# Matmuls whose result is not read: 512 columns in one instruction for four of 128 columns

## The chip, the cores and the metric

One core of a Trainium2 chip runs the whole program in one launch. The metric is the device time of one execution in microseconds (us). TensorE appears in the profile as PE (matmuls) and PEld (the loads of their stationary operand), VectorE as DVE, ScalarE as ACT, GpSimd as POOL, SyncE, which issues most transfers, as SP.

## The reference

Attention over 8 batches of 8 heads (576 tokens, 64 dims each) with a window of 32, plain for heads 0 to 3 and dilated by 4 for heads 4 to 7, and behind it a mixture of 8 experts: each token goes to the expert with the highest logit.

```python
scores = scale * np.matmul(q, k.transpose(0, 1, 3, 2))
scores = np.where(masks[None, :, :, :], scores, -1000000000.0)
scores = scores - np.max(scores, axis=-1, keepdims=True)
attn = np.exp(scores)
attn = attn / (np.sum(attn, axis=-1, keepdims=True) + 1e-09)
attn_out = np.matmul(attn, v)
...
x = attn_out.transpose(0, 2, 1, 3).reshape(B * S, H * D)      # 4608 x 512
logits = x @ w_gate
expert_idx = np.argmax(logits, axis=1)
gate_w = softmax(logits)[np.arange(N), expert_idx]
...
for e in range(E):
    h = np.maximum(x_sorted[lo:hi] @ w1[e], 0.0)              # 512 -> 1024
    y_sorted[lo:hi] = h @ w2[e]                               # 1024 -> 512
return gate_w[:, None] * y_sorted[inv_perm]
```

Everything is float32. No matmul that this change touches has a result that enters the output.

## The kernel before, in words

The work is cut into units of two heads of one batch (32 units). A unit runs through these steps: q and k are loaded and turned by DVE (lines 581 to 596), PE makes the scores block by block (line 659), DVE scales and masks them out of PSUM (line 679) and takes the smallest (691), ACT makes the exponentials and their sums (700), DVE inverts the sums (710, 712), POOL multiplies (716), PE turns the weights (726), ACT or DVE copies them to SBUF as eT (983), and PE multiplies by v (753, 764) into a tile xo that ACT or DVE copies to xT (775, 777). After a batch, a routing stage makes logits (1068, 1082), ranks (1112, 1115) and token rows (1045), and POOL writes the rows to a bucket in DRAM (527). The experts' work follows: some slots of 128 tokens early, between the units of later batches (first layer line 1475, second layer 1491), and after the last batch pairs of slots (lines 1604 to 1640), three single slots and 14 short ones (1742, 1769).

No engine's queue follows the written order of the code. A planner (class Plan) holds all steps with a cost, an engine, the buffers taken and a rank, and emits them one at a time; the order it makes is then pinned for each engine. The planner also models TensorE's clock, and where PE would sit idle before a step it puts matmuls in whose result is not read. It works out how many (m, at most 12) from the idle time and the constant FILL = 0.22 us for each, sets plan.owed = m, and calls ahead(name) when a PSUM tile is free early:

```python
m = max(min(self.MOST, int(idle / us)), self.WARMING if cold and begin < at else 0)
if m > 0:
    self.owed, self.free[e] = m, begin
    if name:
        self.fill(name)
```

The function unread(to) (line 804) emits the owed matmuls: each multiplies the constant tile idle (128x128 ones, written by POOL on line 801) by itself into the first 128 columns of the PSUM tile that the next real step will write. It is called with a fresh tile by bank (line 544), two_banks (729) and ahead (809). The planner stops filling when the first expert slot comes (plan.until), so all of these matmuls lie in the first 118 us. In the trace they stand under line 806, with the names scores, ahead, xo and weights of the tile written.

The kernel's 86 unread matmuls stand in 26 runs of 1 to 12: 12, 12, then runs of 1 to 3, then one of 11, one of 7, one of 4, and runs of 1 to 3 between and after.

Of the kernel before, what the change touches and what calls it, by code (L numbers as in the profile page):

```python
# [357 lines left out]
def kernel(  # L358
# [10 lines left out]
    nc = tc.nc  # L369
# [168 lines left out]
    coming = {}  # L538

    def banks(tag, name):  # L540
        n, bufs = (1024, 1) if tag == "two" else (512, 2)
        return psum.tile([128, n], F32, tag=tag, name=name, bufs=bufs)

    def bank(name, *dims, tag="misc"):
        t = coming.pop(tag, None) or banks(tag, name)
        unread(t[:, 0:128])
        if len(dims) < 2:
            return t[:, 0 : dims[0]] if dims else t
        return t[:, 0 : dims[0] * dims[1]].rearrange("p (a b) -> p a b", a=dims[0])
# [48 lines left out]
    def turn_pe(p, n, m):  # L598

        tp = bank("turned", 6, 64)  # L600
        for c in range(6):
            for r in range(2):
                rows = slice(64 * r, 64 * r + 64)
                nc.tensor.matmul(
                    tp[rows, c], lhsT=raws[p][rows, RUN * n + 6 * m + c], rhs=ident[rows, rows],
                    start=True, stop=True,
                )
        return tp
# [21 lines left out]
    def scores(i, banks):  # L630

        sc = [[bank("scores", tag=t) for t in two] for two in banks]
        parts = [heads_qk(i + u) for u in range(len(sc))]
        G = len(parts[0][0])
# [88 lines left out]
    def weights(ev, g):  # L723
        tp = bank("weights", 4, 128)
        for c in range(3):
            nc.tensor.transpose(tp[0:KB, c], ev[:, 3 * g + c], ident)  # L726
        return tp

    def two_banks(name):
        two = coming.pop("two", None) or banks("two", name)  # L730
        unread(two[:, 0:128])
        return two.rearrange("p (h x) -> p h x", h=2)

    def summed(eT, ty, hp):
        half_s = S // 2
        xo = two_banks("xo")
        if ty == 1:
            for n in range(NB + 1):
# [44 lines left out]
    for i in range(2):  # L783
        a = E * CAP + 128 * i
        wrote_bucket(nc.gpsimd.dma_start(bucket[a : a + 128], blank), 0)
    plan = Plan(0.7)
# [13 lines left out]
    idle = cpool.tile([128, 128], F32, name="idle")  # L800
# [1 line left out]
    plan.others = [(name, ring[name]) for name in ("slot", "two", "s")]  # L802

    def unread(to):
        for _ in range(plan.owed):
            nc.tensor.matmul(to, lhsT=idle, rhs=idle, start=True, stop=True)
        plan.owed = 0

    def ahead(name):
        if name not in coming:  # L810
            coming[name] = banks(name, "ahead")
        unread(coming[name][:, 0:128])

    plan.fill = ahead

# [206 lines left out]
    def route(b, hx, parts, other):  # L1022
# [15 lines left out]
        def to_rows(g):  # L1038

            pv = two_banks("xrow").rearrange("p h (g t x) -> p h t g x", g=4, t=2)  # L1040
            tiles = range(2 * g, min(2 * g + 2, NT))
            for i in tiles:
                for h in range(2):
                    for ty in range(2):
                        nc.tensor.transpose(
                            pv[:, i - 2 * g, ty].rearrange("p (h g) (r x) -> p h r g x", h=2, r=2)[:, h],
                            xT[:, 2 * ty + h, TT * i : TT * i + TT],
                            ident,
                        )
            R["pv", g] = pv  # L1050
# [12 lines left out]
        def parts_of_logits():  # L1063

            lp = two_banks("lp")[:, :, 0 : PAD // 2]
            for g in range(2):
                for c in range(4):
                    nc.tensor.matmul(
                        lp[32 * c : 32 * c + 32, g], lhsT=gate_w[:, c],
                        rhs=xT[:, c, PAD // 2 * g : PAD // 2 * g + PAD // 2],  # L1070
                        start=True, stop=True,
                    )
            R["lp"] = lp
# [1237 lines left out]
```

## Time and profile before

| | us |
|---|---|
| median of 3 runs | 731.18 |
| lowest, highest | 730.61, 737.0 |
| the profiled execution, its own time | 732.32 |
| its span, first to last instruction | 730.5 |
| mean granted TensorE clock | 0.981 |

A run of the same program can differ from the next by several us (730.61 to 737.0). The profiled execution lies 1.14 us above the median, and 1.82 us of its time lie outside its span. Times in rows are counted from the start of the span. In a row of a timeline, the first number is the start and the second the length of a group of like instructions; "[2.89 <-issue]" is idle time of the engine in front of it in which it waited for nothing that the profile shows. A float32 matmul of this kernel leaves two records on PE and two on PEld: line 1491 runs 88 times in the code and has 176 records.

### The profile page before, as it was taken

The numbers are of one execution on the slowest core, as the hardware profiler recorded it, in microseconds if no ns is written. First come the engines' busy times: TensorE is split into PE (matmuls) and PEld (weight loads), VectorE is DVE, ScalarE is ACT, GpSimd is POOL, SyncE is SP. The second block draws the span as 40 slices with busy tenths as digits, with TensorE's granted clock in tenths as the row PEclk, the third lists the DMA queues.
The fourth block names the chain that finished last, engine by engine and source line by source line (L and its number), as shares of the span: only waits on it lengthen the run. The fifth ranks groups of instructions, "written<-read, shape, count | busy, mean of one in ns | idle before, by whom it ended". The sixth has DMA issues, their size and how long they took to land. (4 is left out here: it accounts for less than half of the span.)

```text
span 730.5 us, 21652 instructions
## 1 busy us (share of the span) xinstructions
PE 696.5 (95%) x8520; PEld 584.0 (80%) x8520; DVE 431.7 (59%) x963; ACT 285.9 (39%) x906; POOL 283.1 (39%) x461
## 2 busy tenths in 40 slices
PE   5789999899999999999999999999999999999996
PEld 4678888768778678767987898878989887889894
DVE  7788877767777531754576555417565653455640
ACT  2598877748777764211120211211211212211210
POOL 1135254225343435356064352452542512552511
PEclk9699999999999999999999999999999999999999
DMA  9999977956676985184979569775997759965301
GB/s 267 331 268 313 346 195 209 319 164 177 154 172 156 262 273 185 62 305 99 395 201 348 163 210 395 217 245 157 373 372 223 222 179 385 401 244 198 131 20 48
DMA packets 117326, 171.32 MB, mean 235 GB/s; under 512 B 45628, under 2 KB 69950, under 8 KB 116704
## 3 DMA queue, kind: packets, MB, share of 16 engines
q1 hardware_dynamic: 109712, 149.55, 65.9%
q0 software_dynamic: 6352, 19.69, 7.2%
q8 instruction: 69, 1.13, 0.7%
q10 hardware_dynamic: 1152, 0.61, 0.3%
q14 instruction: 41, 0.34, 0.2%
HBM read 196.27 MB, written 20.22 MB: 296 GB/s over the span
## 5 line engine op out<-in xcount | busy, mean ns | idle before, releaser
L700 ACT ACTIVATE e<-e,lo 128x96 f32<-128x96 f32 x288 | 104.1, 368 | 11.9 <-DVE lo L691 11.9
L716 POOL TENSOR_TENSOR e<-e,rec 128x864 f32<-128x864 f32 x32 | 52.4, 1637 | 103.9 <-DVE rec L712 76.3
L1491 PE MATMUL py<-w,h 128*128 128x512 f32 x176 | 83.8, 611 | 0.9 <-issue 0.9
L1475 PE MATMUL ph<-xt,w 128*128 128x128 f32 x672 | 81.5, 276 | 0.0
L1475 PEld LDWEIGHTS ph<-xt,w 128*128 128x128 f32 x672 | 78.2, 192 | 2.5 <-issue 2.1
L659 PE MATMUL scores<-kT,qT 32*64 32x96 f32 (+2 forms) x2168 | 57.9, 257 | 15.0 <-issue 8.7
L527 POOL DMA_INDIRECT bucket<-rows,idx x40 | 39.4, 985 | 76.5 <-issue 13.9
L659 PEld LDWEIGHTS scores<-kT,qT 32*64 32x64 f32 (+2 forms) x2168 | 48.1, 134 | 22.8 <-issue 17.1
L1491 PEld LDWEIGHTS py<-w,h 128*128 128x128 f32 x176 | 31.6, 193 | 31.1 <-issue 30.6
L679 DVE SCALAR_TENSOR_TENSOR e<-scores,cst 128x384 f32<-128x384 f32 x122 | 43.9, 397 | 20.0 <-PE scores L659 8.6
L700 ACT ACTIVATION_READ_ACCUMULATOR e<-e,lo 128x1 f32 x288 | 55.6, 193 | 0.0
L1678 POOL DMA_INDIRECT out_dram<-y,top x22 | 24.5, 1112 | 79.4 <-ACT y L1659 75.0
L1604 POOL TENSOR_TENSOR v<-w 128x1024 f32<-128x1024 f32 x11 | 27.5, 2498 | 71.1 <-PE late_two L1629 63.7
L983 ACT COPY eT<-weights 96x384 f32<-96x384 f32 x94 | 42.0, 479 | 23.3 <-PE weights L726 19.9
L726 PE MATMUL weights<-cst,e 128*96 128x128 f32 x288 | 45.4, 285 | 3.1 <-POOL e L716 1.1
L1659 ACT ACTIVATE y<-y,gtp 128x512 f32<-128x512 f32 x22 | 15.0, 717 | 81.4 <-DVE y L1640 81.3
L726 PEld LDWEIGHTS weights<-cst,e 128*96 128x96 f32 x288 | 31.3, 131 | 15.6 <-issue 6.7
L1623 PE MATMUL pp<-late_rows,v 128*128 128x128 f32 x352 | 43.3, 276 | 0.0
L1623 PEld LDWEIGHTS pp<-late_rows,v 128*128 128x128 f32 x352 | 41.0, 192 | 1.2 <-issue 0.8
L1629 PE MATMUL pp<-w,h 128*128 128x256 f32 x176 | 41.9, 381 | 0.0
L1640 DVE TENSOR_TENSOR y<-pp,y 128x256 f32<-128x256 f32 x44 | 18.6, 423 | 39.4 <-PE pp L1629 35.2
L1640 DVE TENSOR_TENSOR h<-late_two,h 128x512 f32<-128x512 f32 x11 | 7.6, 688 | 57.0 <-PE late_two L1623 57.0
(223 smaller groups left out, 1454.2 us busy)
## 6 DMA issues: line engine op xcount, KB each, us to landing
w<-in_moe_w_dram SPq DMA_DIRECT2D x40, 2048.0 KB
raw<-in_moe_w_dram SPq DMA_DIRECT2D x42, 1024.0 KB
qT<-in_moe_w_dram SPq DMA_DIRECT2D x28, 512.0 KB
w<-in_moe_w_dram SPq DMA_DIRECT2D x8, 1024.0 KB
raw<-in_q_dram SPq DMA_DIRECT2D x14, 576.0 KB
raw<-in_k_dram SPq DMA_DIRECT2D x14, 576.0 KB
v<-in_v_dram SPq DMA_DIRECT2D x7, 864.0 KB
xT<-bucket SPq DMA_DIRECT2D x44, 128.0 KB
```

The source lines that it names most:

```text
L527: nc.gpsimd.indirect_dma_start(out=bucket, out_offset=bass.IndirectOffsetOnAxis(ap=idx, axis=0), in_=rows, in_offset=None, bounds_check=NR ...
L659: nc.tensor.matmul(two[r][row : row + rows, KB * c : KB * c + KB], lhsT=qs, rhs=ks, start=g == 0, stop=g == G - 1,)
L679: nc.vector.scalar_tensor_tensor(out=to, in0=at, scalar=-SCALE, in1=of, op0=OP.mult, op1=OP.add,)
L700: nc.scalar.activation(out=ev[:, c], in_=ev[:, c], func=AF.Exp, bias=lo[:, c : c + 1], scale=-1.0, accum_out=den[:, c : c + 1],)
L716: nc.gpsimd.tensor_tensor(out=ev, in0=ev, in1=rec.unsqueeze(2).broadcast_to([128, NC, KB]), op=OP.mult)
L726: nc.tensor.transpose(tp[0:KB, c], ev[:, 3 * g + c], ident)
L983: copier(e)(S_["eT"][:, 3 * g : 3 * g + 3], S_["w", g][0:KB, 0:3])
L1475: nc.tensor.matmul(ph[:, f % 4], lhsT=w1s[wbuf[j[0:2]]][:, c, 128 * f : 128 * f + 128], rhs=xt[:, c], start=c == 0, stop=c == 3,)
L1491: nc.tensor.matmul(py, lhsT=h[:, f], rhs=w2s[wbuf[j[0:2]]][:, f], start=f == 0, stop=f == 7)
L1604: (nc.gpsimd if engine == "POOL" else nc.vector).tensor_tensor(out=to, in0=a, in1=b, op=OP.subtract)
L1623: nc.tensor.matmul(to[:, f], lhsT=w[:, c, 128 * f : 128 * f + 128], rhs=x[:, c], start=c == 0, stop=c == 1,)
L1629: nc.tensor.matmul(to[:, 0:256], lhsT=x[:, f], rhs=w[:, f], start=f == 0, stop=f == 3)
```

## The change

unread emits plan.owed // 4 matmuls of 512 columns, whose moving operand is the tile idle read four times by a stride of zero, and then plan.owed % 4 of the old ones of 128 columns. The callers hand over 512 columns of the tile instead of 128. The planner's counts and costs are as they were.

```diff
@@ bank @@
-        unread(t[:, 0:128])
+        unread(t[:, 0:512])
@@ two_banks @@
-        unread(two[:, 0:128])
+        unread(two[:, 0:512])
@@ unread @@
     def unread(to):
-        for _ in range(plan.owed):
-            nc.tensor.matmul(to, lhsT=idle, rhs=idle, start=True, stop=True)
+        four = idle.unsqueeze(1).broadcast_to([128, 4, 128])
+        for _ in range(plan.owed // 4):
+            nc.tensor.matmul(
+                to.rearrange("p (a b) -> p a b", a=4), lhsT=idle, rhs=four, start=True, stop=True
+            )
+        for _ in range(plan.owed % 4):
+            nc.tensor.matmul(to[:, 0:128], lhsT=idle, rhs=idle, start=True, stop=True)
         plan.owed = 0
@@ ahead @@
-        unread(coming[name][:, 0:128])
+        unread(coming[name][:, 0:512])
```

Only runs of four and more change: five of the 26. On DVE, ACT, POOL and SP every instruction stands where it stood. On PE, the head of the program (scores and ahead are the tiles written, kT and qT the turned k and q, cst the constants, e and eT the weights before and after they are turned, v_71 a part of v):

```order
L806 MATMUL scores<-idle 128x128 x12
L659 MATMUL scores<-kT_70,qT 64x96 x72
L806 MATMUL ahead<-idle 128x128 x12
L659 MATMUL scores<-kT_70,qT 64x96 x64
L659 MATMUL scores<-kT_70,qT 32x96 x16
L726 MATMUL weights<-cst,e 96x128 x12
```

```order
L807 MATMUL scores<-idle 128x512 x3
L659 MATMUL scores<-kT_70,qT 64x96 x72
L807 MATMUL ahead<-idle 128x512 x3
L659 MATMUL scores<-kT_70,qT 64x96 x64
L659 MATMUL scores<-kT_70,qT 32x96 x16
L726 MATMUL weights<-cst,e 96x128 x12
```

The first of these two pieces is the kernel before, the second the changed one: each run of 12 has become 3, and the real matmuls between them stand in the same order. Further on PE, where the turned weights of a unit and the ranks of the third batch stand (weights, ahead and xo are the tiles written, front and idle the operands of the count), first of the kernel before:

```order
L806 MATMUL weights<-idle 128x128 x11
L726 MATMUL weights<-cst,e 96x128 x9
...
L806 MATMUL ahead<-idle 128x128 x7
L1112 MATMUL rank<-front,idle 128x48
L1115 MATMUL rank<-oh,cst 128x40
L726 MATMUL weights<-cst,e 96x128 x3
L806 MATMUL xo<-idle 128x128 x4
L764 MATMUL xo<-eT,v_71 64x64 x8
```

and of the changed kernel, whose lines behind 803 stand five further down:

```order
L807 MATMUL weights<-idle 128x512 x2
L811 MATMUL weights<-idle 128x128 x3
L726 MATMUL weights<-cst,e 96x128 x9
...
L807 MATMUL ahead<-idle 128x512
L811 MATMUL ahead<-idle 128x128 x3
L1117 MATMUL rank<-front,idle 128x48
L1120 MATMUL rank<-oh,cst 128x40
L726 MATMUL weights<-cst,e 96x128 x3
L807 MATMUL xo<-idle 128x512
L764 MATMUL xo<-eT,v_71 64x64 x8
```

Here 11 have become 2 and 3, 7 have become 1 and 3, and 4 have become 1; everything else is in its old order.

## Rows read from the trace of the kernel before

**Rows 1.** The page, its head: the span, the busy time of each engine with its share and number of instructions, and the queue that brings PE's code, with its packets, MB and share of the 16 DMA engines.

```profile
span 730.5 us, 21652 instructions
PE 696.5 (95%) x8520; PEld 584.0 (80%) x8520; DVE 431.7 (59%) x963; ACT 285.9 (39%) x906; POOL 283.1 (39%) x461
q8 instruction: 69, 1.13, 0.7%
```

**Rows 2.** The instructions of line 806 on PE, those of the first run (its tile is a bank of scores): how many records, the least, median and greatest length of one in ns, and the starts of the first and the last in us.

```profile
L806 PE MATMUL scores<-idle x24: 274/421/579, 4.0 to 8.1; 128*128 128x128 f32 x24
```

**Rows 3.** The timeline of PE, two stretches of like records back to back, of 128 and of 512 columns: start, length, and how many.

```profile
259.46 6.42 PE L1475 MATMUL ph<-xt,w 128*128 128x128 f32 x56
265.72 2.74 PE L1491 MATMUL py<-w,h 128*128 128x512 f32 x6
```

**Rows 4.** The timeline of PE (and of POOL, ACT and DVE where named), the five runs of four and more, and what stands behind each.

```profile
4.04 4.38 PE L806 MATMUL scores<-idle 128*128 128x128 f32 x24 [4.04 <-POOL idle L801]
9.11 0.34 PE L659 MATMUL scores<-kT,qT 32*64 32x96 f32 x8 [0.69 <-DVE kT L581]
12.11 2.94 PE L806 MATMUL ahead<-idle 128*128 128x128 f32 x24
19.11 0.46 PE L659 MATMUL scores<-kT,qT 32*64 32x96 f32 x8 [4.05 <-DVE kT L596]
69.85 2.72 PE L806 MATMUL weights<-idle 128*128 128x128 f32 x22
72.41 0.82 PE L726 MATMUL weights<-cst,e 128*96 128x128 f32 x6
72.99 0.47 ACT L983 COPY eT<-weights 96x384 f32<-96x384 f32 x1
73.52 0.31 PE L726 MATMUL weights<-cst,e 128*96 128x128 f32 x1 [0.29 <-issue]
90.21 1.83 PE L806 MATMUL ahead<-idle 128*128 128x128 f32 x14
91.88 0.32 PE L1112 MATMUL rank<-front,idle 128*128 128x48 f32 x2
92.45 0.20 DVE L1123 TENSOR_TENSOR pick<-rank,oh 128x40 f32<-128x40 f32 x1 [1.14 <-PE rank L1115]
92.59 1.06 PE L806 MATMUL xo<-idle 128*128 128x128 f32 x8
93.58 0.63 PE L764 MATMUL xo<-eT,v 96*64 96x64 f32 x14
```

**Rows 5.** The timeline of PE, the five idle times in front of a matmul of a row of like ones that fall to "issue".

```profile
26.50 0.27 PE L659 MATMUL scores<-kT,qT 32*32 32x96 f32 x1 [2.89 <-issue]
39.66 0.24 PE L659 MATMUL scores<-kT,qT 32*64 32x96 f32 x1 [0.98 <-issue]
50.34 0.27 PE L659 MATMUL scores<-kT,qT 32*32 32x96 f32 x2 [0.86 <-issue]
145.83 0.40 PE L659 MATMUL scores<-kT,qT 32*64 32x96 f32 x9 [3.24 <-issue]
207.55 0.51 PE L753 MATMUL xo<-eT,v 96*64 96x64 f32 x11 [0.39 <-issue]
```

**Rows 6.** Busy time by stretch, each from one of these idle times to the next: stretch and length in us, then busy us and (x instructions) of PE, PEld, DVE, ACT and POOL, granted clock, DMA share, GB/s.

```profile
25.00:39.20 14.20, 11.94 (x254) 10.56 (x255) 9.10 (x14) 8.59 (x36) 1.56 (x1) 0.76 0.90 323
39.20:49.90 10.70, 9.54 (x254) 8.34 (x253) 10.36 (x22) 10.11 (x40) 2.63 (x3) 1.00 1.02 282
49.90:144.00 94.10, 89.04 (x1775) 78.04 (x1776) 77.20 (x196) 78.28 (x299) 40.84 (x84) 1.00 0.93 276
144.00:207.40 63.40, 60.08 (x1017) 46.43 (x1017) 44.03 (x140) 41.36 (x152) 24.99 (x59) 0.97 0.68 179
```

**Rows 7.** The DMA queues in two stretches, 137.0 to 142.8 us (the first row, its only queue) and 142.8 to 143.0 us (the second): packets, MB, and the time of their packets as a share of the 16 engines' time.

```profile
q1 hardware_dynamic: 3289, 1.41, 128.4%
q8 instruction: 1, 0.02, 45.9%
```

**Rows 8.** Busy time by stretch, columns as in rows 6: the instructions that follow the first idle time of rows 5, the last 256 before the fourth, and those that follow the fourth.

```profile
25.00:30.37 5.37, 3.63 (x35) 2.89 (x35) 2.78 (x7) 2.41 (x9) 0.00 (x0) 0.74 1.03 390
137.45:142.58 5.13, 5.13 (x138) 4.46 (x129) 3.89 (x8) 4.78 (x17) 1.63 (x1) 1.00 1.30 228
144.00:147.45 3.45, 1.62 (x59) 1.50 (x61) 0.00 (x0) 0.00 (x0) 0.00 (x0) 0.94 1.00 350
```

**Rows 9.** Busy time by stretch, columns as in rows 6: three short stretches that hold 256 instructions of PE and PEld and some in flight at their edges.

```profile
47.88:51.38 3.50, 2.64 (x146) 1.88 (x140) 2.46 (x5) 3.50 (x17) 1.63 (x1) 1.00 0.82 240
74.31:78.33 4.02, 4.02 (x137) 3.54 (x133) 3.65 (x8) 4.02 (x18) 1.64 (x1) 1.00 1.01 413
105.88:110.24 4.36, 4.16 (x136) 2.94 (x132) 3.31 (x9) 4.36 (x18) 1.63 (x1) 1.00 0.89 302
```

**Rows 10.** Busy time by stretch, columns as in rows 6: two stretches at the low clock.

```profile
27.56:34.39 6.83, 6.59 (x60) 6.03 (x61) 5.56 (x8) 3.51 (x12) 0.00 (x0) 0.50 1.02 408
147.03:150.44 3.41, 3.41 (x36) 1.43 (x35) 2.59 (x4) 0.25 (x1) 1.18 (x1) 0.50 1.09 236
```

**Rows 11.** The waits: who waited for whom, us in total, times, longest. The first row is DVE's between 15 and 60 us, the second is PE's over the span.

```profile
DVE e L679 <- PE weights L726: 2.5, 1, 2.5
PE late_two L1623 <- DVE y L1640: 2.6, 1, 2.6
```

## The prediction, made before the changed kernel was run

> **What bounds the kernel now.** I read the page first, and there the busy shares: PE works in 696.5 of 730.5 us [rows 1], no other engine in more than 59%. So the time is PE's queue: what PE has to do, at which clock, and where it stands still. Then I read the timeline of PE around the unread matmuls [rows 4] to see what each run hides behind, and two stretches of back-to-back matmuls for the price of a column in either form [rows 3]. Last I read PE's idle times by what ended them, because the change takes instructions out of PE's queue and I wanted to know whether their number matters. It does: five idle times inside rows of like matmuls are put down to "issue", 2.89, 0.98, 0.86, 3.24 and 0.39 us, 8.36 us together [rows 5]. The reader should see that nothing the profile knows of is late there: the matmul before and the one behind belong to the same step.
>
> What they are is shown by counting. Between one such idle time and the next lie 254 + 255 = 509, 254 + 253 = 507, 1775 + 1776 = 3551 and 1017 + 1017 = 2034 counted instructions of PE and its weight loads [rows 6]. That is 2, 2, 14 and 8 times 256, less 1% for waits that this view leaves out. PE's code comes by a queue of its own, 69 packets for 1.13 MB, 16.4 KB each [rows 1], and 17,040 instructions over 69 packets are 247 for each. So PE stands at the border of a block of 256 instructions, and the code behind it has not come. Before the longest of them, no packet of that queue ran from 137.0 to 142.8 us, while the other transfers took 128% of the engines' time; the packet began between 142.8 and 143.0, and PE went on at 145.83 [rows 7, 5]. Counting 256 back from that border, the block was entered at about 137.45 (267 instructions to 142.58, some of them in flight at its edges) [rows 8]: it ran 5.1 us, and its successor came 8.4 us after it was entered. Counted back by 256 in the same way, the other four blocks were entered at 20.47, 36.71, 47.40 and 200.81, and their successors came 6.0, 2.95, 2.94 and 6.8 us after that. A block that runs longer than that shows no stall.
>
> **The change part by part. The columns.** A row of 56 records of 128 columns takes 6.42 us and one record 0.28, so one starts (6.42 - 0.28) / 55 = 0.112 us after the other; for 512 columns it is (2.74 - 0.61) / 5 = 0.426 us [rows 3]. A float32 matmul is two records: four old ones take 0.893 us, one new one 0.85. Each of the ten merges (3, 3, 2, 1, 1) gives 0.04 us, 0.4 us in all. I take the line 1491 rate for the new form, which the trace of before does not show with a stride of zero; bounds are 0.85 us on one side and 4 x 0.421, the length at the low clock, on the other [rows 2].
>
> Of the 0.4 us little is on the path. The two runs of 12 end before idle times of 0.69 and 4.05 us in which PE waits for DVE's turned k [rows 4]: six merges, nothing. The run of 11 ends at 72.41, but behind the next two groups PE waits until 73.52 for ACT's copy at 72.99, which follows ACT's own work: nothing. Behind the run of 7 the rank matmul starts at once, and DVE has waited 1.14 us for it; behind the run of 4 the product with v starts at once. Two merges, 0.08 us, are on the path.
>
> The Trainium skill (page "TensorE: Matmul & The Clock Gate", section "Back-to-back issue gap") gives about 81 ns for a matmul of 128 columns in a real stream and 131 for 512. By that ratio a merge would give 0.53 us instead of 0.04, and the last three runs, with their covers, about 1.2 us. The rows go against it: 426 against 112 is close to four to one.
>
> **Clock.** The first run lifts PE's clock: its records take 421 ns at the low clock (1.2 GHz) and 274 at the high one (2.4) [rows 2]. The columns stay the same in number and place, so I give this nothing; the other outcome is a rival below.
>
> **The code.** Ten merges take out 30 matmuls, and each is two records on PE and two on the weight loads: 120 instructions, 36 and 36 in the first 15 us, 24 at 70 us, 12 and 12 at 90 and 93. So from 15 us on every border of a block lies 72 instructions later in the program, from 72 us on 96, from 93 us on 120, about half a block. Each stall of [rows 5] loses its place, and each new border is a new chance of one. I go through them by the time that the block before the new border runs, against the time in which code came (2.9 to 8.4 us).
>
> First stall, 2.89 us at 26.50: the border moves on by 72 instructions, to about 30.37 [rows 8]. Its block was entered at 20.47 and is now entered at 21.3; less the stall it runs 6.2 us. Code that came 6.0 us after the entry is in time: the 2.89 us go. Second and third, 0.98 and 0.86: the blocks ran 2.0 and 2.1 us in the dense scores of four heads. The one becomes a block of 4.5 us (37.2 to 42.6, less the stall), enough for code in 2.95; the other one of 3.50 - 0.86 = 2.6 us [rows 9], which still waits 0.3. Fourth, 3.24: the border moves to 147.45 (59 + 61 = 120 instructions after the stall) [rows 8], which without the stall is 144.2; if the code again lands for 145.83, PE waits 1.6 us, and 1.6 go. Fifth, 0.39: gone. Sum of the old ones: 8.36 become 1.9.
>
> New short blocks: one of 4.02 us before 78.33 and one of 4.36 us before 110.24 [rows 9]. Bounds are 0 (code in 2.9 us) and 4.4 and 4.0 us (code in 8.4 us); I take 0.7 each, nearer to no stall, since the transfers there take 101 and 89% of the engines' time [rows 9] and not 130% as before the stall at 142.6 [rows 8]. Five more blocks of 5.0 to 5.9 us lie between 93 and 220 us: 0 to 3.4 each, taken as 0.2. Sum 2.4 us. PE would stand 4.3 us in place of 8.36.
>
> How much of it reaches the end? The first three lie before 51 us, where DVE, ACT and the loads set the pace as much as PE; DVE waits 2.5 us for PE there [rows 11], so PE is late at least there. I take half of (4.73 - 0.3): 2.2 us. The new stalls count in full, -2.4. The fourth gives 1.6, the fifth 0.4. The stall at 142.6 is followed by a stretch at half clock, 147.03 to 150.44, with PE busy in all of it [rows 10]: with half the stall gone, I take half of its price of 3.41 / 2 = 1.7, 0.85 us. With 0.1 for the merges: 2.2 - 2.4 + 1.6 + 0.4 + 0.85 + 0.1 = 2.75 us. What is late next is the start of the pairs, where PE waits 2.6 us for DVE [rows 11], which itself stands behind a load of weights; about a third of the gain ends there. Left: 1.9 us. From the profiled execution's 732.32 us that makes 730.4; it lies 1.14 us above the median of the runs, so I predict 729.3 for the median.
>
> The Trainium skill (page "Runtime: NRT & Kernel Launch", section "Instruction fetch mechanics") says that code comes in blocks of 256 instructions, the next one while the current one runs, and that crossing a border is mostly hidden. The size agrees with the counts of [rows 6]; "mostly hidden" does not agree with 8.36 us of idle time [rows 5]. By that sentence alone, the term above would be nothing.
>
> **Rivals.** (1) The borders move and nothing reaches the end: the early stalls lie under DVE and the loads, the later ones cancel, or the wait of 2.6 us at the pairs takes up the rest. For it: DMA is busy in 90 to 130% of its time in the first 150 us [rows 6, 8]; against it: from 150 us on PE hardly waits. It leaves the 0.1 us of the merges: 731.1. In the Trainium skill, "mostly hidden" (page "Runtime: NRT & Kernel Launch", section "Instruction fetch mechanics") would make this the case to expect. (2) Slower: the new borders fall worse. The block before 110.24 us runs 4.36 us; if its successor comes as late as at 142.6, 8.4 us after the entry, PE stands 4.0 us, and a stretch at half clock may follow as at 147, 1.7 us. Late code is a matter of the transfers in front of it, 128% at 137 us but 89% here. It decides from code later than 4.4 us plus what the other borders gain. 5.7 us lost for 1.9 won in the sum: 731.2 + 3.8 = 735. (3) Much faster: all 8.36 us reach the end, the cold stretch at 147 goes, and so does the one from 27.56 to 34.39, which follows the first stall and in which PE is busy for 6.59 us, 3.3 of them lost [rows 10]: 8.36 + 1.7 + 3.3 less what new stalls take, 2.4, is 11: 720. (4) The unread matmuls in their new form don't hold the clock: each of the five runs is followed by a stretch of 3.4 us at half clock, 1.7 us each, 8.5 us: 739.7. For it speaks only that the weight loads between them go; against it, that 512-column matmuls of line 1491 run at the high rate [rows 3].
>
> **How the numbers follow.** Forecast, 1 to 5 us faster: 0.47. Rival 1, within 1 us: 0.25. Rival 2, 1 to 7 us slower: 0.20. Rival 3: 0.05. Rival 4: 0.03. About 1%, 7.3 us, is what a measurement of this kernel can tell from no change; the runs of before themselves span 6.4 us. So faster by more than that has rival 3's 0.05, slower by more has rival 4 and the far end of rival 2, 0.05, and the rest, 0.90, is within 1%. The range from 725.8 to 735.0 holds the forecast's 1 to 5 us, rival 1 and most of rival 2; left out are rivals 3 and 4 and the ends of the others, some 0.18. The bounds of the new stalls taken all together would reach further on both sides, but they are separate events.
>
> **What would show it.** In the profile of the changed kernel: 112 records for the unread matmuls in place of 172, twenty of them 0.43 us apart; PE's idle times by "issue" away from the second group of scores of the first units and from 142.6 us, and the ones that are left 256 instructions, or a multiple, apart from each other. The theory is wrong if idle times by "issue" stand at the same matmuls as before, or if their sum falls by some us and the time does not follow though DVE's waits for PE shrink as well. The forecast is wrong if new idle times by "issue" of 4 us or more stand near 78 or 110 us, or if PE's clock falls right behind one of the five runs.

## The result: slower by 0.7%, and the profile after

The changed kernel takes 736.47 us (median of 22 runs), the kernel before 731.26 (22 runs): a ratio of 1.0067, 95% interval 1.0046 to 1.0087. Medians here are over all runs, while ratios leave out the slow ones, more than 1.5% above the fastest of their kernel (three of the changed kernel's 22, none of the kernel before), so that a ratio need not be the quotient of two medians. The prediction said 729.3 with a range to 735.0. The sign was wrong, and the time lies outside the range.

The head of the page of the changed kernel, as in [rows 1]:

```profile
span 734.7 us, 21532 instructions
PE 696.4 (95%) x8460; PEld 580.2 (79%) x8460; DVE 434.7 (59%) x963; ACT 286.8 (39%) x906; POOL 282.4 (38%) x461
q8 instruction: 68, 1.11, 0.6%
```

120 instructions of PE and its weight loads are gone and one code packet with them. PE is busy for 696.4 us, as before. So nothing is lost in what PE does. It stands still longer.

The merged matmuls themselves, in the timeline of PE, the first two runs of [rows 4]:

```profile
4.04 4.26 PE L807 MATMUL scores<-idle 128*128 128x512 f32 x6 [4.04 <-POOL idle L801]
...
12.45 2.84 PE L807 MATMUL ahead<-idle 128*128 128x512 f32 x6
```

Three new matmuls in place of 12 old ones took 4.26 us against 4.38, and 2.84 against 2.94 [rows 4]: 0.03 to 0.04 us for each merge.

The idle times that fall to "issue", in the timeline of PE, which answer to the five of [rows 5] (start, length, what ran, and in brackets the idle time ahead of it):

```profile
27.78 0.80 PE L764 MATMUL ahead<-eT,v 96*64 96x32 f32 x18 [1.11 <-issue]
34.20 0.30 PE L659 MATMUL scores<-kT,qT 32*64 32x96 f32 x3 [0.98 <-issue]
42.28 1.01 PE L753 MATMUL ahead<-eT,v 96*64 96x64 f32 x14 [3.58 <-issue]
54.23 0.73 PE L1073 MATMUL lp<-xT,gate_w 128*32 128x320 f32 x4 [1.49 <-issue]
...
82.10 1.14 PE L659 MATMUL scores<-kT,qT 32*64 32x96 f32 x44 [0.88 <-issue]
...
115.09 0.85 PE L659 MATMUL scores<-kT,qT 32*64 32x96 f32 x22 [0.99 <-issue]
...
140.38 0.31 PE L659 MATMUL scores<-kT,qT 32*64 32x96 f32 x1 [1.41 <-issue]
...
149.70 0.97 PE L753 MATMUL xo<-eT,v 96*64 96x64 f32 x25 [0.61 <-issue]
...
222.80 0.89 PE L659 MATMUL scores<-kT,qT 32*64 32x96 f32 x32 [0.32 <-issue]
```

Nine in place of five, 11.4 us in place of 8.4, none at a matmul where one stood before. Four of them lie before 60 us, 7.2 us together, where the kernel before had 4.7. The worst one, read by stretch (columns as in [rows 6]): the block that it follows, the idle time, and what comes behind.

```profile
34.20:38.70 4.50, 4.45 (x127) 3.94 (x127) 3.86 (x11) 3.71 (x18) 1.80 (x2) 1.00 1.32 217
38.70:42.28 3.58, 0.00 (x2) 0.00 (x0) 3.50 (x8) 1.12 (x6) 0.74 (x1) 0.83 1.03 242
41.05:47.88 6.83, 5.60 (x42) 5.27 (x41) 3.60 (x6) 2.63 (x6) 0.00 (x0) 0.50 0.86 313
```

The block of 256 instructions ran 4.50 us, just as the prediction had it. Its successor came 8.1 us after the entry (42.28 less 34.20) instead of 2.95. The DMA queues say what went on meanwhile; the first row is the only queue between 34.2 and 39.5 us, the second is the code queue between 39.5 and 40.8 us (packets, MB, share of 16 engines):

```profile
q1 hardware_dynamic: 3136, 1.12, 133.5%
...
q8 instruction: 1, 0.02, 6.6%
```

For 5.3 us after the entry the loads took 133% of the engines' time and no code packet ran. PE's clock then fell: 6.83 us at 0.50, in which PE worked for 5.60 us, so 2.8 us were lost to the low level, in place of the stretch behind the first stall of [rows 10].

How the loss builds up is seen by comparing the starts of the same DVE instructions in both profiled executions. The changed kernel is 4.2 us ahead at 37 us, 2.8 behind at 61, 3.6 at 110, 7.6 at 128, 9.8 at 140, 5.5 at 160 to 196, 2.5 at 237 to 353 and 1.6 from 390 to 594 us. From 636 us to the end it is 4.3 us behind.

The step between 110 and 128 us comes with the idle time of 0.99 us at 115.09: a stretch at the low clock follows it, in which PE works without a pause, so that half of it, 3.4 us, is lost. Where the lag shrinks, it is the kernel before that stands: for 3.24 us at 145.83, with the low stretch behind it [rows 5, 10], and for 0.39 us at 207.55, with another low stretch behind. The two stretches that neither the rows nor the prediction show, first of the changed kernel, then of the kernel before (columns as in [rows 6]):

```profile
116.10:122.93 6.83, 6.83 (x35) 6.75 (x34) 3.11 (x12) 3.48 (x9) 0.80 (x1) 0.50 0.39 82
...
208.50:211.90 3.40, 3.40 (x5) 1.34 (x5) 3.29 (x9) 2.02 (x7) 1.29 (x1) 0.50 0.56 133
```

The last 2.7 us lie where the prediction did not look. Behind 600 us PE's timeline has idle times that the kernel before did not have:

```profile
617.69 0.65 PE L1774 MATMUL py_s<-raw,own 128*32 128x128 f32 x16 [0.51 <-DMA raw<-in_moe_w_dram]
...
619.01 0.43 PE L1774 MATMUL py_s<-qT,own 128*32 128x128 f32 x8 [0.68 <-DMA qT<-in_moe_w_dram]
620.50 0.43 PE L1774 MATMUL py_s<-qT,own 128*32 128x128 f32 x8 [1.05 <-DMA qT<-in_moe_w_dram]
```

PE waits for weights whose loads SP issued late, because SP stood before the fourth row of the load ahead of them. The timeline of SP there, of the changed kernel (start, time from the first of its four issues to the last):

```profile
595.77 6.57 SPq L1440 DMA_DIRECT2D xT<-bucket  x4
602.54 0.39 SPq L1448 DMA_DIRECT2D gtp<-bucket  x1
604.34 1.85 SPq L1736 DMA_DIRECT2D raw<-in_moe_w_dram  x3
```

and of the kernel before:

```profile
594.21 3.99 SPq L1435 DMA_DIRECT2D xT<-bucket  x4
598.40 0.39 SPq L1443 DMA_DIRECT2D gtp<-bucket  x1
600.21 2.03 SPq L1731 DMA_DIRECT2D raw<-in_moe_w_dram  x3
```

SP takes 6.57 us for what took 3.99, and 2.6 us are what is lost there. What SP waits for is in its waits between 590 and 606 us, first of the changed kernel, then of the kernel before: the landing of a load of weights that it issued ahead of this row.

```profile
SPq L1440 <- DMA w<-in_moe_w_dram: 4.4, 1, 4.4
...
SPq L1435 <- DMA w<-in_moe_w_dram: 1.8, 1, 1.8
```

### The profile page after: what moved, and what is told of

It reads as the page before. It is cut to its first block, busy times and chain, and to the rows that moved or that the text cites. A ratio compares the mean times of both kernels' runs of the same rounds, so it can differ in the third digit from the quotient of the medians.

```text
span 734.7 us, 21532 instructions
## 1 busy us (share of the span) xinstructions
PE 696.4 (95%) x8460; PEld 580.2 (79%) x8460; DVE 434.7 (59%) x963; ACT 286.8 (39%) x906; POOL 282.4 (38%) x461
## 3 DMA queue, kind: packets, MB, share of 16 engines
q8 instruction: 68, 1.11, 0.6%
## 5 line engine op out<-in xcount | busy, mean ns | idle before, releaser
L1496 PE MATMUL py<-w,h 128*128 128x512 f32 x176 | 82.1, 601 | 0.9 <-issue 0.9
L659 PE MATMUL scores<-kT,qT 32*64 32x96 f32 (+2 forms) x2168 | 56.0, 254 | 11.4 <-issue 4.7
L1683 POOL DMA_INDIRECT out_dram<-own,toq x14 | 14.4, 1028 | 70.9 <-ACT own L1785 69.5
```

The lines of the kernel that those rows point to most:

```text
L659: nc.tensor.matmul(two[r][row : row + rows, KB * c : KB * c + KB], lhsT=qs, rhs=ks, start=g == 0, stop=g == G - 1,)
L1496: nc.tensor.matmul(py, lhsT=h[:, f], rhs=w2s[wbuf[j[0:2]]][:, f], start=f == 0, stop=f == 7)
L1683: i = nc.gpsimd.indirect_dma_start(out=out, out_offset=bass.IndirectOffsetOnAxis(ap=to, axis=0), in_=y, in_offset=None, bounds_check=out.s ...
```

## The experiments

All ratios are against the kernel before, run on the same chip beside it, with 95% intervals. Most edits use one helper: a matmul of 32 by 32 that nobody reads, 4 instructions on PE and its weight loads, 64 of them in 1.93 us:

```
+    def small(to, x, n):
+        for i in range(n):
+            r = c = 32 * (i % 4)
+            nc.tensor.matmul(
+                to[c : c + 32, 0:32], lhsT=x[r : r + 32, 0:32], rhs=x[r : r + 32, 0:32],
+                start=True, stop=True,
+            )
```

**1. The changed kernel with its old number of instructions.** Each merged matmul is followed by three small ones, so that every border is where it was:

```
                 to.rearrange("p (a b) -> p a b", a=4), lhsT=idle, rhs=four, start=True, stop=True
             )
+            small(to, idle, 3)
```

> The changed kernel, with three small matmuls (32 by 32, 32 columns, not read) behind each of the ten 512-column ones, so that PE has as many instructions at every place as before. Theory 1 (the time moves because the borders of PE's code blocks of 256 instructions fall at other matmuls, and the new form itself is worth nothing): idle times by 'issue' at the same matmuls as before (26.5, 39.7, 50.3, 145.8, 207.6 us), and 731.3 us, at most 1 us more for the small ones behind the last three runs. Theory 2 (the 512-column form itself costs, by the clock or by holding PE): 736.5 us, as the changed kernel.

It took 732.79 us, ratio 1.0002 (0.9974 to 1.0029). The loss is gone, and PE's idle times are back in their places, at the first three matmuls of [rows 5]:

```profile
27.20 0.36 PE L659 MATMUL scores<-kT,qT 32*32 32x96 f32 x1 [3.36 <-issue]
...
40.85 0.24 PE L659 MATMUL scores<-kT,qT 32*64 32x96 f32 x1 [2.71 <-issue]
...
52.92 0.27 PE L659 MATMUL scores<-kT,qT 32*32 32x96 f32 x2 [0.97 <-issue]
```

So the loss comes from the number of instructions, not from the form of the matmul, as far as an interval of 0.3% either way can tell. The row also warns: at the same places this execution stood 7.0 us before 60 us where [rows 5] has 4.7. The length of a stall differs from one execution to the next; its place doesn't. And of those 7.0 us, about as many as in the changed kernel, little reached the end: by DVE's starts this execution is 2.5 us behind at 61 us, 0.8 at 237 and 0.5 from 450 us on.

**2 to 4, 7 and 8. The kernel before with its borders moved.** Small matmuls at the head of PE's queue, with nothing merged; 16, 34, 48, 56 or 64 of them, which are 64, 136, 192, 224 or 256 instructions:

```
+    at_head = [34]
...
     def unread(to):
+        if at_head:
+            small(to, kTs[0][:, 0, 0:WIN], at_head.pop())
```

> The kernel before, its unread matmuls of 128 columns as they were, with 34 small matmuls (136 instructions of PE and its loads) at the head of PE's queue, where it waits 4 us anyway. Every border lies 136 instructions earlier in the program, which modulo 256 is 120 later, as in the changed kernel from 93 us on. Theory 1: about 736 us (734 to 738), with idle times by 'issue' at the changed kernel's places behind 93 us (in front of 115, 140 and 150 us) and not at 145.8. Theory 2: 731.3 us, since no 512-column matmul is in it.

> The control: the kernel before with 64 small matmuls at the head, 256 instructions, one whole block. Theory 1: every border stands where it stood, so the idle times by 'issue' are at the same matmuls as before and the time is 731.3 us (within 1). If more instructions or an earlier use of PE by themselves cost or gave time, it would differ from 731.3 here most of all.

> The kernel before with 16 small matmuls at the head, 64 instructions, a quarter of a block. Theory 1: borders 64 instructions earlier, idle times by 'issue' at new matmuls, a time different from 731.3 in either direction (727 to 738). Theory 2: 731.3 us.

> The kernel before with 48 small matmuls at the head (192 instructions, borders 64 instructions later in the program). If the length of the block in front of a border decides by itself (a block under 4.5 us stands still), this place loses less than before: 728 us. If it is decided by when code comes, that is by the transfers in front of it, the sum does not follow from the blocks' lengths, and the time may be 727 to 738 us. A theory by which the borders don't matter gives 731.3 us.

> The kernel before with 56 small matmuls at the head (224 instructions, borders 32 instructions later in the program), to see how far the time follows the place of the borders, and whether a place beats the kernel before. By the blocks' lengths alone 730 us; by the transfers, 727 to 738 us; without any effect of the borders 731.3 us.

What was measured, with the two kernels and run 1 for comparison; the idle times are those of over 0.2 us at block borders in the one profiled execution, and "late wait" says whether PE waits for the weights' loads some 23 us after the place in SP's queue shown above:

| instructions more, ahead of most borders | median us | ratio | idle at borders, us | late wait |
|---|---|---|---|---|
| before, 0 | 731.26 | 1 | 8.4 | no |
| run 1, 0 | 732.79 | 1.0002 (0.9974 to 1.0029) | 11.3 | no |
| run 4, 64 | 733.99 | 1.0035 (1.0004 to 1.0066) | 14.1 | yes |
| run 2, 136 | 738.30 | 1.0060 (1.0020 to 1.0100) | 10.4 | yes |
| changed, -120, or 136 less 256 | 736.47 | 1.0067 (1.0046 to 1.0087) | 11.4 | yes |
| run 7, 192 | 736.21 | 1.0038 (1.0008 to 1.0067) | 8.5 | yes |
| run 8, 224 | 734.03 | 0.9989 (0.9951 to 1.0027) | 9.0 | no |
| run 3, 256 | 732.91 | 1.0018 (0.9987 to 1.0049) | 9.5 | no |

Runs 1 to 4 and runs 7 and 8 come from two chips, on which the kernel before had 731.48 and 732.73 us: rows are to be compared by their ratios. The profiled executions of runs 2, 4 to 6, 9 and 12 to 14 took 3 to 6 us longer than the medians of their kernels, so their idle times don't belong to the medians beside them.

Run 2 is the changed kernel's loss without the change: the borders behind 93 us stand where they stand there, and it is as much slower, though its profiled execution is only 0.8 us behind at 61 us. Run 3, whose 256 instructions put every border back, is the control: the 1.9 us of the matmuls themselves hardly show. Run 7 is a miss: by the lengths of the blocks alone it should have been the fastest, 728 us, and it was slower. A block's length does not tell whether its successor is late. The wide range that runs 4, 7 and 8 were given for the other case, 727 to 738 us, tests little: hardly any result would have left it. The sixteen profiled executions of this study have 93 idle times of over 0.5 us behind 20 us that fall to "issue"; 89 of them stand at the same instruction of 256, and PE goes on 1.2 to 1.7 us after its code packet has landed. What differs is how long the packet waits.

**5. Only the borders behind 400 us put back**, in the changed kernel; what goes before is as changed:

```
+        if (layer, i, n) == (0, 2, 1):
+            small(to, idle, 30)
```

> The changed kernel with 30 small matmuls (120 instructions) in front of the first product of the third pair of slots, at about 400 us, where PE waits 3 us for DVE behind that product anyway. From there on every border of a code block stands where it stood before the change; before 400 us nothing is altered. In the changed kernel's profile 2.7 of the 4.2 us come at 617 to 620 us, where PE waits for the weights of a short slot, after SP stood 4.4 us in front of a transfer at 597.6 while PE's code packet ran in the tail of a load of weights. Theory 1b (that packet's place makes the load late): the waits at 617 to 620 us go, and the time is 733.8 us (732.5 to 735). Rival 1c (the wait comes from being 1.5 us later at 590 us, whatever the borders): waits as in the changed kernel, 736.5 us.

735.03 us, ratio 1.0038 (1.0008 to 1.0068): by the ratios 2.1 us of the 4.9 are gone, though this interval still overlaps the changed kernel's. In its profile PE has no wait for a DMA between 600 and 650 us, and SP takes 4.42 us:

```profile
603.19 4.42 SPq L1448 DMA_DIRECT2D xT<-bucket  x4
```

In this execution DVE came to that place 9.0 us later than in the kernel before, against 1.6 in the changed kernel. So coming late is not what brings the wait.

**6. Only the borders behind 400 us moved**, in the kernel before: the same edit with 34.

> The kernel before with 34 small matmuls (136 instructions, 120 later modulo 256) at the same place at about 400 us: the borders stand as in the changed kernel from there on, and as before up to there. Theory 1b: PE waits for the weights of a short slot near 617 us, and the time is 734 us (733 to 735.5). Rival 1c: no such wait, 731.3 us.

The trace shows the wait, at the same matmuls, and SP standing:

```profile
619.18 0.43 PE L1779 MATMUL py_s<-qT,own 128*32 128x128 f32 x8 [1.25 <-DMA qT<-in_moe_w_dram]
620.57 0.42 PE L1779 MATMUL py_s<-qT,own 128*32 128x128 f32 x8 [0.97 <-DMA qT<-in_moe_w_dram]
```

```profile
595.72 5.90 SPq L1443 DMA_DIRECT2D xT<-bucket  x4
```

The time, 733.63 us, ratio 1.0009 (0.9981 to 1.0037), moved less than the 2.7 us expected; the interval reaches just so far and to no change as well. As a time it settles nothing. As a trace it does: over all sixteen executions, a code packet began 0.6 to 2.9 us after DVE's instruction at this place in seven, and those are the seven with the wait (1.2 to 2.6 us in sum); in the other nine it began 6 to 7 us ahead and again 5 to 9 us behind, and none has it.

The traces also tell more of what SP waits for. The load of weights that SP waits for, 2 MB, tells of its landing in sixteen parts. Fifteen of them have landed 7.5 to 8.1 us after its issue in all sixteen executions. The sixteenth comes 9.6 to 10.7 us after it in the seven with the wait, where a code packet began 4.6 to 6.9 us after the issue, and 7.6 to 8.4 us after it in the other nine, where the packet began 9 us or more after the issue. So one part in sixteen of this load comes 1.5 to 2.6 us after the others where a code packet runs inside the load, and SP's row waits for that part.

**9 and 10. Less load in front of the early code.** In both kernels only 128 columns of the first weights are loaded; the rest is set to zero, so these two leave out a part of the computation:

```
-            dst[e][:, m * half : m * half + m],
-            src[e].rearrange("(c l) f -> l c f", l=128)[:, m * half : m * half + m],
+            dst[e][:, m * half : m * half + m, 0:128],
+            src[e].rearrange("(c l) f -> l c f", l=128)[:, m * half : m * half + m, 0:128],
...
+    for w in (*w1s, *w2s):
+        nc.gpsimd.memset(w[:, :, 128:], 0.0)
```

> The kernel before with only 128 columns of each row of the first weights loaded (128 KB in place of 1024 KB for each w1 half, 256 KB in place of 1024 KB for each w2 half); the rest of those weights is set to zero by GpSimd at the start, so the short slots that use them compute with zeros. PE's instructions and their number stay as they were; what changes is that some 4 MB of load less stand in the first 60 us. Theory A (code comes late because it shares the DMA engines with loads that were issued ahead of it): PE's idle times with the releaser 'issue' between 20 and 60 us, 2.89 + 0.98 + 0.86 = 4.73 us in the kernel before, fall below 2 us in sum; the run gains about as much, 728 us. Theory B (the lag belongs to the code queue itself, whatever is loaded): the sum stays within 1 us of 4.7, at the same instructions, and the time stays at 731 to 732 us.

> The changed kernel with the same cut of the first weights (the same part of the computation is left out). Theory A: its idle times with the releaser 'issue' between 20 and 60 us, 1.11 + 0.98 + 3.58 + 1.49 = 7.16 us, fall below 2 us in sum, so that the border at 34 us is no longer worse than those of the kernel before and DVE stands within 1 us of the other run at 60 us, where it was 2.8 us behind. The time falls to about 731 us (736.5 less 5), and the rest of the difference to the other kernel of this call comes behind 600 us from the wait for the late load. Theory B: 7.2 us of stalls as now, DVE 2 to 3 us behind at 60 us, time 736.

Ratios 0.9964 (0.9942 to 0.9986) and 1.0008 (0.9973 to 1.0042). The times moved as theory A had it, by -0.4% from the kernel before and by -0.6% from the changed one, but the idle times did not: before 60 us they were 7.8 us in the one and 5.2 us in the other, not under 2. By stretch, in the first of them (columns as in [rows 6]):

```profile
20.00:30.00 10.00, 6.27 (x156) 4.84 (x156) 5.84 (x13) 3.08 (x14) 3.26 (x2) 0.69 1.02 280
30.00:40.00 10.00, 7.70 (x243) 6.66 (x242) 9.34 (x18) 9.09 (x42) 1.63 (x1) 0.97 0.89 235
```

The share of the DMA engines is 1.02 and 0.89, in the kernel before 1.08 and 0.87 in the same stretches: the loads behind in the queue moved up and filled the room. The edit did not do what it was meant to do, so these runs neither show nor refute theory A.

**11. More load in front of code, where there was none.**

```
+    more_to = [nc.dram_tensor(f"more_{i}", (128, 4608), F32, kind="Internal").ap() for i in range(2)]
+
+    def more(i):
+        a = q[0, 0]
+        nc.sync.dma_start(more_to[i], bass.AP(a.tensor, a.offset, [[4608, 128], [1, 4608]]))
...
+        if (p, n) == (13, 1):
+            more(0)
...
+        if (p, n) == (14, 0):
+            more(1)
```

> The kernel before with two transfers more that nobody reads or waits for: 2.36 MB of q to a scratch space in DRAM, issued by SP behind the k load at 150.6 us and behind the q load at 172.8 to 174.5 us. The engines' instructions stay as they were. In the kernel before, PE entered code blocks there at 154.99 us (DMA share over the next 4 us 0.01, the code packet was under way already) and at 178.29 us (share 0.44, the packet 1.33 us later); the second of these blocks lasted 4.3 us and no stall followed. Theory A (a code packet stands behind the bytes in transfer): the packets of the blocks entered inside the added transfers come 2.5 to 5 us after the entry, and at about 183 us an idle time with the releaser 'issue' of 1.5 to 3.5 us appears that the kernel before had not; the time rises by 0 to 3 us. Theory B (the wait belongs to the code queue): packets at -0.3 and 1.3 us as before, no stall between 152 and 190 us, time 731 to 732.

The block entered at 156.74 us got its packet 2.60 us after the entry, where it had been under way already. The block entered at 180.07 got it 4.7 us after the entry, where that had been 1.33. The DMA queues: the first row is the only queue that ran from 180.0 to 184.7 us, the second is the code queue between 184.7 and 186.0 us:

```profile
q1 hardware_dynamic: 80, 1.96, 115.5%
...
q8 instruction: 1, 0.02, 5.0%
```

And at the end of that block PE stands, which it did not do in the kernel before:

```profile
187.26 1.38 PE L669 MATMUL scores<-kT,qT 32*64 32x96 f32 x26 [2.62 <-issue]
```

with a stretch at 0.59 of the clock behind it:

```profile
187.00:190.50 3.50, 3.24 (x42) 1.47 (x42) 2.06 (x4) 0.00 (x0) 0.41 (x1) 0.59 1.03 224
```

The packets came as theory A expected, and not as theory B did. The time rose by more than the 0 to 3 us expected: 738.48 us, ratio 1.0072 (1.0036 to 1.0107). The stall and the low clock behind it cost 4.5 us by DVE's starts at 191 us, and the k load, which SP issued 5 us later than before, stood behind them.

**12. The early loads moved away**, in the changed kernel, with every instruction of the engines in its place:

```
+LATER = ((), (), (), (0,), (1,), (2,), (3, 4), (5, 6, 7))
...
-            add("SP", 0.4, lambda e, i=i: first_weights(i), rank=FIRST_W + STEP_W * i, moved=3.1)
+            add("SP", 0.4, lambda e, i=i: [first_weights(m) for m in LATER[i]], rank=FIRST_W + STEP_W * i, moved=3.1)
```

> The changed kernel with the same instructions on every engine, but the eight 1 MB loads of the first weights issued later: the first three places of SP's order issue none, so that the loads that stood at 24.6, 27.0 and 41.2 us come at 52 us and later, and the last ones stand in the place of 84.8 us. Theory A: the DMA share between 26 and 50 us falls, and with it the stalls that 'issue' ended between 20 and 60 us, from 7.16 us to 2.5 to 5 us (the version with these loads cut small had 5.17); DVE stands 2 to 4 us earlier at 60 us than in the changed kernel, and the time falls to 732 to 735. Theory B: 7.2 us of stalls and 736 us as now.

733.94 us, ratio 1.0031 (0.9990 to 1.0072). The four early idle times of the changed kernel, at the same matmuls:

```profile
26.97 0.80 PE L765 MATMUL ahead<-eT,v 96*64 96x32 f32 x18 [0.30 <-issue]
...
33.66 0.30 PE L660 MATMUL scores<-kT,qT 32*64 32x96 f32 x3 [1.25 <-issue]
...
39.55 0.62 PE L754 MATMUL ahead<-eT,v 96*64 96x64 f32 x14 [1.58 <-issue]
50.58 0.73 PE L1074 MATMUL lp<-xT,gate_w 128*32 128x320 f32 x4 [1.57 <-issue]
```

4.7 us in place of 7.2; the one of 3.58 has become 1.58. At 61 us DVE is 0.9 us ahead of the kernel before, 3.7 us better than the changed kernel, and the wait behind 600 us is still there. But the gain did not last in this execution: at 140 us DVE is 9.5 us behind, after a stall of 1.76 us at 113.01, and 2.3 to 2.7 us behind from 237 to 594 us, where the changed kernel was 2.5 to 1.6 behind. The interval holds no loss as well as the changed kernel's.

**13 and 14. Both parts taken away, and the loads alone.** Run 13 is the changed kernel with the edits of runs 5 and 12, run 14 the kernel before with that of run 12.

> The changed kernel with both: the first weights issued later, as in the run before, and 30 small matmuls that nobody reads at about 400 us, which put the code borders behind them back to their old places. Theory (two parts, both of them code against transfers): no wait for a DMA at 617 to 621 us, stalls before 60 us of 4 to 5 us, and a time within 0.3% of the kernel before: 736.5 - 2.5 - 2.7 = 731. Rival (a third part of the loss lies elsewhere, in the merged matmuls or in a clock that rises later): it stays above 1.004 of the kernel before.

> The kernel before with the first weights issued later in the same way; nothing else. If the loads moved away help wherever they stood in front of code: stalls before 60 us of 2 to 4 us in place of 4.73, time 729 to 730. If they only happened to stand in front of the changed kernel's borders: stalls within 1 us of 4.7 and 731 to 732.

Run 13: 730.61 us, ratio 0.9992 (0.9966 to 1.0019); 4.9 us of idle times before 60 us, no wait for the late weights, SP as in the kernel before:

```profile
596.53 3.98 SPq L1449 DMA_DIRECT2D xT<-bucket  x4
```

The whole loss is gone, with the merged matmuls in place, and here the interval lies clear of the changed kernel's (1.0046 to 1.0087), which those of runs 5 and 12, with one part each, did not. That both parts were needed is not shown as firmly: the intervals of runs 5 and 13 just overlap. Run 14: 730.59 us, ratio 0.9987 (0.9959 to 1.0016), 4.4 us of idle times before 60 us; about 1 us better than the kernel before, which the interval does not separate from nothing. Neither run is an improvement that these measurements can show.

## Why the prediction was wrong, step by step

- **Blocks of 256, and 120 instructions that move the borders: right.** Runs 1, 2 and 3 show that the number of instructions ahead of a border, counted in rests of 256, makes the difference, and the merged form none that these runs can show.
- **The merges, 0.04 us each: right** (4.26 us for 4.38). The Trainium skill (page "TensorE: Matmul & The Clock Gate", section "Back-to-back issue gap") gives about 81 ns for a matmul of 128 columns and 131 for one of 512, and an estimate from these of 0.53 us for each merge; the rows do not agree with that here.
- **The clock held by the new form: right.** None of the changed kernel's low stretches stands right behind one of the five runs. The three that the kernel before does not have, from 41.1, 116.1 and 140.0 us, begin inside a stall or 1 us behind one.
- **The step that failed: "against the time in which code came".** The prediction took the time from entry to code as belonging to the place. For the second stall it wrote: "The one becomes a block of 4.5 us ..., enough for code in 2.95". The block came out at 4.50 us; its code took 8.1. The gain of the step before it was real, 4.2 us at 37 us, and with it this block came into a burst of loads: it was entered at 34.20 us in place of 36.71. In runs 12 and 13, which move the loads away, it was entered at 33.66 and 34.44 us, and the stall of 3.58 us was 1.58 and 1.65. The third block, foreseen with 0.3 us, waited 1.49 (code 4.5 us after the entry in place of 2.94). The first, foreseen as gone, waited 1.11. With one of 0.98 us at 34.20, which the prediction did not have, the early stalls, 0.3 us in the sum, were 7.2. How much of this reached the end is not shown: run 12 takes 2.5 us of it away, but its interval holds the changed kernel's loss as well as none, and run 1 had as much idle time there and no loss that shows.
- **The new stalls at 78 and 110 us, 0.7 us each: right in place and size**, 0.88 and 0.99. What the sum put at nothing is the low clock behind the second, 3.4 us between 116.10 and 122.93 us; the prediction counted a low stretch only as a gain, behind the stall at 142.6. The fourth stall, foreseen with 1.6 at its moved border, did not come there: that block was entered at 154.37 without a wait, and the two borders ahead of it had 1.41 and 0.61. The fifth is gone, as foreseen, and 0.32 us stand at the border behind it; it was worth more than its 0.4, since the low stretch behind it, 1.7 us, went too.
- **"What is late next is the start of the pairs": not seen.** A third of the gain was to end there, in PE's wait of 2.6 us for DVE; in the changed kernel PE waits 3.1 us at that place. From 196 to 390 us the lag of 5.5 us shrank to 1.6, most of it between 205 and 212 us, where the kernel before has its own stalls and low stretch.

```profile
PE late_two L1628 <- DVE y L1645: 3.1, 1, 3.1
```

- **What lies behind 600 us: missing.** The prediction had no border there at all, since the blocks are long. But a code packet also stands in the way of others: by it the wait for weights came in, 2.7 us in the profile, 2.1 by the ratios of run 5.
- **The rivals.** Rival 2, "the new borders fall worse", is what happened, with 735 us for 736.5. It put the price at 110 us, as a stall of 4.0 us and 1.7 for the clock; the place had a stall of 0.99 and lost 3.4 to the clock. But its sum has neither the stalls before 60 us nor the wait at 617 us, so that it came so near is in part luck. Rival 1 is refuted by the ratio, rival 4 by the traces and, as to the time, by run 1.

The Trainium skill (page "Runtime: NRT & Kernel Launch", section "Instruction fetch mechanics") calls the crossing of a block mostly hidden. The sixteen executions have 8.3 to 14.1 us of idle time at such borders each. For most borders the sentence holds: 89 of some 1050 entries behind 20 us had an idle time of over 0.5 us. Between 20 and 60 us, where it was 47 of 102, it doesn't.

Open is why a code packet of 1 us holds up one part of a load by 1.5 to 2.6 us; that the packet's place decides whether PE waits is shown by runs 5 and 6 and by the sixteen traces. How the 4.9 us divide is not settled either. Run 5 gives 2.1 us to the wait behind 600 us, with an interval that overlaps the changed kernel's; what each stall before 230 us is worth at the end is open, since the stalls of a single execution do not put the times of the table in order.

## What to carry to other kernels

In a kernel whose bottleneck engine runs dense, short instructions while loads keep the DMA engines full, any edit ahead of that place moves the borders of its code blocks, and that alone was worth -0.1 to +0.7% here: before a small gain or loss is put down to an edit, run a version padded to the old number of instructions. To forecast a stall, compare the length of a block with the time that its code needs under the loads of the moment when it will be entered, not with the time that it needed where it stood. And a load that is to be out of the way of code has to be issued later, not merely made smaller: in runs 9 and 10 the loads behind it in the queue moved up.

## What the runs showed of the hardware

The wait of a code packet grows with the load on the DMA engines. Over the sixteen executions I took the entries into a block and the code packet that goes with each, 860 pairs, and the share of the 16 DMA engines that other transfers took in the 4 us from the entry:

| share of the DMA engines | entries | entry to start of the packet, median us | 10% to 90% |
|---|---|---|---|
| under 0.3 | 79 | 0.3 | -0.4 to 1.2 |
| 0.3 to 0.7 | 166 | 0.8 | 0.2 to 1.8 |
| 0.7 to 0.9 | 114 | 1.8 | -0.1 to 2.9 |
| 0.9 to 1.1 | 405 | 2.7 | 0.8 to 4.0 |
| 1.1 to 1.3 | 79 | 3.1 | 1.0 to 4.7 |
| over 1.3 | 17 | 5.0 | 3.2 to 5.5 |

With about 1.1 us for the packet and 1.4 us until PE goes on, code is there some 2.8 us after the entry when the engines are idle, and 5 to 8 us when they are full. These sums are estimates from the table's medians. Some 200 entries whose packet had begun more than 0.5 us before them are not in the table; with them the medians of the rows are lower, -0.5, 0.5, 1.5, 2.4, 3.3 and 5.0 us, in the same order. Among these only run 11 adds load by hand; the table is what the traces have side by side.
